# A gated linear attention with an FFN behind it: one table of calls in another order

## The chip, the cores and the metric

The kernel runs on one core of one Trainium2 chip. The metric is the device time of the whole program in microseconds, with smaller times better; it is compared by the median of several runs. Engines are named as in the profile: PE is TensorE, DVE is VectorE, ACT is ScalarE, POOL is GpSimd, and SP is SyncE, which does nothing here but start DMAs.

## The reference

The first half is a recurrence over 768 positions in each of 4 batches and 8 heads, with 48 complex gates per head. The second half is a plain FFN on its output.

```python
mag = np.sqrt(a_re * a_re + a_im * a_im)
scale = np.minimum(mag, 0.999) / (mag + 1e-06)
a_re_n, a_im_n = (a_re * scale, a_im * scale)
for t in range(S):
    S_re = ar * S_re - ai * S_im + kv      # kv = outer(k_t, v_t)
    S_im = ar * S_im + ai * S_re           # with the S_re of step t-1
    y[:, :, t] = einsum('bhd,bhde->bhe', q[:, :, t], S_re)
x = y.transpose(0, 2, 1, 3).reshape(B * S, H * D)     # 3072 x 384
h = x @ w_in                                          # 384 -> 2048
out = (h * (1.0 / (1.0 + np.exp(-h)))) @ w_out        # 2048 -> 384
```

## The kernel before

**Tiling.** The positions are cut into 24 chunks of 128, numbered n, in such an order that chunks n and n + 4 follow each other in the same batch. Two chunks make a pair p of 256 tokens, the unit of the FFN; there are 12 pairs. The FFN's 2048 columns are cut into 8 blocks jp.

**One chunk of attention.** The gates of a pair (logarithm of the magnitude, angle) come out of eleven steps G0 to Ga on ACT and DVE. The last of them, `gates_angle`, writes the tile th on the DVE (lines 431 and 433). For a chunk that has one before it in its batch, `carried` (line 441) adds the last row of the chunk before to th by an accumulating DMA on POOL's queue, th<-last. PE then forms running sums of both, ACT and DVE make sines, cosines and decays of them, and q and k are rotated and scaled on the DVE (line 551). `squared` (line 587) transposes the result in blocks of 32 into the tile sq, and `homed` (line 593) brings these blocks to their places in the tile T by twelve DMAs, T<-sq: six issued by SP and six by POOL. `weights` (line 606) multiplies a<-T on PE, `masked` (line 614) applies the causal mask on the DVE, and `output` (lines 633 and 636) gives y. `state` (lines 693 and 704) forms the chunk's contribution to the recurrent state, and `state_homed` (line 722) brings it into place by twelve more DMAs, S<-ssq, in the same way on both queues. `ends_of` stores a chunk's last decays by SP (line 522, ends<-eq) and loads them in another layout by two DMAs on POOL (line 525, dec<-ends), which wait for that store.

```python
def homed(n):
    to = home(n).rearrange("d w h a x -> d (w h) a x")
    for b in range(NB):
        for a in range(NA):
            (nc.gpsimd if a % 2 else nc.sync).dma_start(
                out=to[ts(b, Q), :, a],
                in_=X[n]["sq"][ts(a, Q), b].rearrange("p w h x -> p (w h) x"))
```

**One pair of the FFN.** `put` and `third_of` (lines 677, 681 and 645) bring y to the transposed input xT. From pair 3 on each product is split into three of lower precision: ACT makes the rounded copy xH of xT (`x_head`, line 772), the DVE the remainders xL and xD (lines 834 and 838), and `hidden` (line 762) multiplies xH by coarse, xL by fine and xD by mixed. For most blocks fine is loaded again by SP (`v_loaded`, line 817, fine<-w_firsts), and the DVE makes mixed of it and coarse (line 834). `silu` (line 312) gives g. ACT and DVE split g into head, tail and gd (lines 896, 834 and 838), and `result` (line 935; line 917 for the first pairs) multiplies them by three forms of w_out, one of which is loaded by SP (`w_loaded`, line 875, diff<-w_diffs). Loaded fine and diff tiles share a ring of three buffers; mixed has one.

**What sets the order.** The program is built by a table of calls, a string from line 1058 to 1204, in which each word is a call and its arguments: `td:18` is `homed(18)`, `xh:3` is `x_head(3)`, `h:6.1` is `hidden(6, 1)`. It runs under a manual schedule, so each engine and each queue executes its instructions exactly in the order in which the table issues them, and an instruction that waits holds back all those behind it on its engine or queue. Idle multiplications (`warm`) are calls of the table too; their results are not used. One thing depends on the order besides: ACT holds one set of function tables at a time. `special` (line 309) emits an ACT_TABLE_LOAD (line 306) when the set in place has not got the function that comes next.

Of the kernel before, what the change touches and what calls it, by code (L numbers as in the profile page):

```python
# [70 lines left out]
def kernel(  # L71
# [985 lines left out]
    with tc.manual_schedule():  # L1057
        for x in """
                warm:30 re:0 e0:0 im:0 e1:0 e2:0 re:1g im:1 e4:0 e0:1 im:2g e1:1 e3:0 im:3g e2:1
                e4:1 e6:0 e5:0 q:0g e6:1 e7:0 e7:1 e8:0 e8:1 L:0 re:2g e3:1 re:3g warm:20 exp:0  # L1060
                at:0.0 e5:1 F: L:1 an:0.0 at:0.1 v:0g phase:0 k:0g an:0.1 G0:1 phase:1 k:1g F: rd:0
                G5:1 R: v:2g turn:0 rd:1 trig:0 warm:34 turn:1 trig:1 dk:0 q:1g exp:1 G8:1 rk:0.0
                v:1g dq:0 rk:0.1 rq:0.0 H: G1:1 s:0 rq:0.1 dk:1 t:0.0 t:0.2 G7:1 ends:0 sm:1 J:
                T:0.0 T:0.2 last:0 t:0.1 dq:1 H: t:0.3 hold: rk:1.1 T:0.1 rq:1.1 G3:1 ends:1 q:2g
                rk:1.0 T:0.3 G6:1 w:0.1 t:1.1 m:0.1 G2:1 s:1 rq:1.0 G4:1 t:1.3 T:1.1 S:0 G9:1
                thirds:0 lk:1 w:0.0 L:3 exp:3 Ga:1 L:2 T:1.3 exp:2 t:1.2 phase:2 F: q:3g S:1 sm:0
                thirds:1 k:2g m:0.0 w:1.1 dq:2 rd:2 y:0 t:1.0 F: turn:2 trig:2 last:2 lk:0 H: im:4g
                dk:2 T:1.2 rq:2.0 rk:2.0 T:1.0 phase:3 rk:2.1 t:2.2 re:4g w:1.0 ends:2 F: R: x:0 R:
                rd:3 t:2.0 m:1.1 rq:2.1 T:2.0 turn:3 re:5g s:2 m:1.0 R: H: trig:3 y:1 k:3g F: T:2.2
                J: J: x:1 t:2.3 J: R: im:5g F: T:2.3 t:2.1 h:0.0 R: T:2.1 h:0.1 dq:3 S:2 rq:3.1  # L1070
                g:0.0 w:2.0 rq:3.0 dk:3 H: J: H: v:3g F: t:3.3 rk:3.1 t:3.2 rk:3.0 G0:2 w:2.1 G5:2
                G8:2 F: g:0.1 t:3.1 T:3.3 thirds:3 F: T:3.2 m:2.0 m:2.1 J: G1:2 H: thirds:2 t:3.0
                r:0.0 R: ends:3 J: T:3.0 R: y:2 H: T:3.1 H: last:1 x:2 G7:2 F: w:3.1 R: F: w:3.0
                G3:2 R: m:3.1 m:3.0 r:0.1 H: y:3 J: J: G2:2 J: x:3 R: F: v:4g G6:2 H: s:3 G4:2 F:
                G9:2 H: R: H: h:1.0 R: S:3 F: last:3 Ga:2 J: H: h:1.1 g:1.0 g:1.1 F: carried:4 J:
                R: L:4 R: r:1.0 F: J: r:1.1 h:1.2 h:0.2 phase:4 F: R: k:4g H: F: exp:4 J: H: J:
                g:1.2 R: R: sm:2 h:0.3 H: H: rd:4 F: carried:5 H: turn:4 J: g:0.2 F: R: F: q:4g J:
                h:1.3 trig:4 H: F: H: q:5g J: H: H: ends:4 R: F: J: J: dq:4 g:0.3 last:4 Q:4 lk:2
                R: dk:4 J: R: K:4 F: phase:5 r:1.2 H: L:5 R: rd:5 im:6g tk:4 g:1.3 R: r:0.2 turn:5
                F: h:1.4 J: H: exp:5 F: F: tq:4 k:5g H: J: R: g:1.4 h:0.4 R: J: J: J: H: g:0.4  # L1080
                r:0.3 h:1.5 R: R: h:0.5 ends:5 dq:5 H: J: J: wq:0 re:6g last:5 wq:1 wd:0 g:1.5
                r:1.3 g:0.5 im:7g ws:0 re:7g s:4 we:0 trig:5 wd:1 r:1.4 td:4 wq:2 dk:5 S:4 G0:3
                h:0.7 K:5 k:6g k:7g we:1 G5:3 Q:5 w:4.0 w:4.1 g:0.7 G1:3 h:0.6 tk:5 m:4.0 wk:0 tq:5
# [294 lines left out]
```

## Time and profile before

| | us |
|---|---|
| median of three runs (666.83 to 668.81) | 668.57 |
| the profiled execution, own time | 666.95 |
| its span | 665.2 |
| PE busy (92% of the span) | 613.8 |
| DVE busy (75%) | 495.6 |
| ACT busy (69%) | 458.0 |
| POOL busy (33%) | 222.4 |

The span is the time from the first to the last instruction in the profile; the execution's own time holds 1.75 us more around it. SP does nothing but start DMAs, which is not counted as busy. The granted clock of PE is given as a share of its full speed: 1.00 is 2.4 GHz and 0.50 is 1.2 GHz. In the lists of waits each line names the engine and line that waited, what released it, the us in total, the number of waits and the longest. In a timeline each line has its start in us from the span's start, the us it took, the engine, the line and the tiles (out<-in), with the idle time before it in brackets.

### The profile page before, as it was taken

What the parts mean: (1) busy time and instruction counts of PE and PEld (TensorE: products, weight loads), DVE (VectorE), ACT (ScalarE), POOL (GpSimd) and SP (SyncE); (2) the same over time, 40 slices, a digit from 0 to 9 for tenths busy, and PEclk for the clock granted to TensorE, in tenths of its full rate; (3) what the DMA queues carried; (4) which work ended last, traced back from release to release, by engine and by line L of the source; (5) the groups of instructions that cost most, each with busy time, mean ns of one, the idle gap of its engine ahead of it and who ended that gap; (6) DMA issues with size and microseconds to landing.
All of it is one profiled execution on the core that took longest, in us unless ns stands there. A gap on an engine that the chain in (4) does not pass through costs nothing.

```text
span 665.2 us, 12665 instructions
## 1 busy us (share of the span) xinstructions
PE 613.8 (92%) x4356; PEld 550.9 (83%) x4356; DVE 495.6 (75%) x763; ACT 458.0 (69%) x718; POOL 222.4 (33%) x389
## 2 busy tenths in 40 slices
PE   6799999999998797879899997999799999999995
PEld 4588777776887687869898997999799999999995
DVE  4879969885697898568799897688597887665353
ACT  7988856996999987537789677578568653343221
POOL 7242314462135422712442653225533033200000
PEclk8979999999999798989999998999799999999999
...
GB/s 177 178 85 204 188 257 169 139 174 213 170 194 225 177 178 143 189 180 157 177 180 151 181 122 223 115 191 158 128 114 220 199 187 160 157 231 156 184 147 95
DMA packets 168452, 114.27 MB, mean 172 GB/s; under 512 B 137804, under 2 KB 143504, under 8 KB 168384
## 3 DMA queue, kind: packets, MB, share of 16 engines
...
HBM read 83.50 MB, written 11.08 MB: 142 GB/s over the span
## 4 chain that ended last, share of the span: by engine, by line
PE 56%; ACT 19%; DMA 9%; DVE 6%; issue 6%; SPq 2%; POOL 1%; ACTq 0%; DVEq 0%; POOLq 0%
PE h L762 16%; PE o L935 16%; PE a L606 5%; PE h L755 4%; ACT L306 4%; ACT s L312 4%; PE o L917 4%; ACT mag L312 2%; PE y L633 2%; DMA T<-sq 2%; PE y L636 2%; DMA fine<-w_firsts 1%; ACT head L896 1%; PE s L693 1%; ACT g L312 1%
## 5 line engine op out<-in xcount | busy, mean ns | idle before, releaser
L593 POOL DMA_DIRECT2D T<-sq x120 | 70.8, 628 | 59.6 <-PE o L935 16.9
L306 ACT ACT_TABLE_LOAD x69 | 88.5, 1283 | 2.7 <-ACT ot L948 1.2
L312 ACT ACTIVATE g<-h 128x512 f32<-128x512 f32 x96 | 56.5, 594 | 45.2 <-PE h L762 34.5
L896 ACT ACTIVATE head<-g 128x512 fp32r<-128x512 f32 x75 | 47.2, 629 | 54.3 <-PE o L935 37.7
L525 POOL DMA_DIRECT2D dec<-ends x48 | 32.0, 694 | 156.0 <-DMA ends<-eq 149.8
L834 DVE SCALAR_TENSOR_TENSOR tail<-head,g 128x512 fp32r<-128x512 f32 x75 | 51.3, 684 | 42.5 <-ACT head L896 27.2
L762 PE MATMUL h<-xD,mixed 128*128 128x256 f32 x432 | 76.9, 287 | 5.0 <-DVE mixed L834 3.8
L762 PE MATMUL h<-xH,coarse 128*128 128x256 f32 x432 | 77.8, 289 | 2.0 <-ACT xH L772 1.4
L762 PE MATMUL h<-xL,fine 128*128 128x256 f32 x432 | 76.9, 287 | 1.4 <-DVE xL L834 1.4
L935 PE MATMUL o<-diff,gd 128*128 128x384 f32 x300 | 67.3, 346 | 5.1 <-DMA diff<-w_diffs 4.1
L606 PE MATMUL a<-T 96*128 96x128 f32 x384 | 56.5, 297 | 16.6 <-DMA xT<-y 4.2
L606 PEld LDWEIGHTS a<-T 96*128 96x128 f32 x384 | 52.7, 208 | 20.4 <-issue 8.5
L935 PE MATMUL o<-coarse,head 128*128 128x384 f32 x300 | 68.8, 351 | 0.4 <-ACT ot L948 0.4
L762 PEld LDWEIGHTS h<-xD,mixed 128*128 128x128 f32 x432 | 63.3, 194 | 6.1 <-DVE mixed L834 4.6
L762 PEld LDWEIGHTS h<-xH,coarse 128*128 128x128 f32 x432 | 64.2, 193 | 4.9 <-ACT g L312 2.0
L935 PE MATMUL o<-fine,tail 128*128 128x384 f32 x300 | 65.3, 340 | 0.3 <-DVE tail L834 0.3
L755 PE MATMUL h<-xT,w 128*128 128x256 f32 x288 | 65.3, 381 | 0.3 <-ACT g L312 0.2
L762 PEld LDWEIGHTS h<-xL,fine 128*128 128x128 f32 x432 | 63.2, 193 | 1.6 <-DVE xL L834 1.6
L755 PEld LDWEIGHTS h<-xT,w 128*128 128x128 f32 x288 | 54.0, 190 | 9.9 <-ACT g L312 1.8
L935 PEld LDWEIGHTS o<-diff,gd 128*128 128x128 f32 x300 | 53.3, 190 | 8.6 <-issue 4.5
L838 DVE SCALAR_TENSOR_TENSOR gd<-tail,g 128x512 fp32r<-128x512 f32 x75 | 51.5, 687 | 6.7 <-PE o L935 3.0
L722 POOL DMA_DIRECT2D S<-ssq x84 | 46.4, 614 | 27.4 <-DVE ssq L711 21.0
...
## 6 DMA issues: line engine op xcount, KB each, us to landing
...
```

The source lines that it names most:

```text
L306: nc.scalar.preload_act_table_set(SETS[of][0])
L312: nc.scalar.activation(out=out, in_=in_, func=func, **kw)
L525: nc.gpsimd.dma_start(out=x["dec"][a * D:(a + 1) * D], in_=ends[n].rearrange("(h d) -> d h", d=D))
L593: (nc.gpsimd if a % 2 else nc.sync).dma_start(out=to[ts(b, Q), :, a], in_=X[n]["sq"][ts(a, Q), b].rearrange("p w h x -> p (w h) x"))
L606: nc.tensor.matmul(ps[:, h], lhsT=x["kT"][hh * HH + h], rhs=x["qT"][hh * HH + h], start=True, stop=True)
L722: (nc.gpsimd if g % 2 else nc.sync).dma_start(out=to[ts(b, Q), r, :, e], in_=sq[ts(g, Q), :, b, 0:e.stop - e.start])
L755: nc.tensor.matmul(ps[:, ji], lhsT=of_first(w1, dc, jp * 2 + ji), rhs=A[p]["xT"][:, dc], start=(dc == 0), stop=(dc == ND - 1))
L762: nc.tensor.matmul(ps[:, ji], lhsT=w(dc, ji), rhs=x[:, dc], start=(f == 0 and dc == 0), stop=(f == len(forms) - 1 and dc == ND - 1))
L834: nc.vector.scalar_tensor_tensor(out=dst, in0=head.bitcast(F32), scalar=-FINER / MORE, in1=whole, op0=ALU.mult, op1=ALU.add)
L838: nc.vector.scalar_tensor_tensor(out=dst, in0=tail.bitcast(F32), scalar=MORE / FINER, in1=whole, op0=ALU.mult, op1=ALU.subtract)
L896: nc.scalar.mul(g_form(p, jp, "head"), A[p]["g", jp], MORE * SPLIT / FINER)
L935: nc.tensor.matmul(to, lhsT=left[:, ji, ts(m, C)], rhs=right(ji), start=(first_ and ji == 0 and n == 0), stop=(last_ and ji == 1 and n == 2))
```

## The change

The table's words are put in another order, from its first line to its last. No call is added, taken out or given another argument, and no buffer is changed. One line of it and one of the new order, the two in which `td:18` stands, show how they read:

```diff
@@ -1056,149 +1056,148 @@
-                carried:21 vx:6.6 gb:7.4 gc:7.4 g:6.5 x:17 ht:20 K:19 ut:20 r:7.4 td:18 dq:19 Q:19
...
+                exp:19 q:19 G1:10 g:6.4 h:7.4 k:19 lw:6.4 ends:19 td:18 G7:10 gr:7.3 w:17.1 vx:6.5
...
```

All engines get the same instructions but for the table loads of line 306, which follow from the order of ACT's functions: there were 69, and there are 73. Three places show how the rows moved. After a tile's name stands its number, and then its size; x6 is six DMAs in a row.

**POOL's queue, where chunk 18's tile T is filled.** T18<-sq18 are POOL's six of its twelve transfers, dec19 the loads of chunk 19's decays, th10 the angles of pair 10, and S20 and S21 states. Before:

```order
L722 DMA S21_5004<-ssq17_4946 32x4x16 x6
L441 DMA th10_4821<-last 1x16x24
L525 DMA dec19_5080<-ends 48x8x1 x2
L441 DMA th10_4821<-last 1x16x24
L593 DMA T18_5145<-sq18_5039 32x8x64 x6
L177 MEMSET v19_5220 128x16
```

And in the new order:

```order
L722 DMA S20_4855<-ssq16_4558 32x4x16 x6
L525 DMA dec19_4957<-ends 48x8x1 x2
L593 DMA T18_4960<-sq18_4878 32x8x64 x6
L441 DMA th10_4810<-last 1x16x24
L722 DMA S21_5156<-ssq17_4674 32x4x16 x6
L441 DMA th10_4810<-last 1x16x24
```

T18 went ahead of both accumulations into th10, and stands right behind the loads of dec19.

**SP's queue, where chunk 16's tile T is filled.** T16<-sq16 are SP's six transfers, S19<-ssq15 six of a state, fine6_1 a weight for block 1 of pair 6, and xT7 an FFN input. Before:

```order
L645 DMA xT7_4090<-y3_7_4092 16x256 x3
L875 DMA diff4_7_4291<-w_diffs 128x768
L497 DMA last<-turn17_4133 1x384
L722 DMA S19_4303<-ssq15_4125 32x4x32 x6
L522 DMA ends<-eq17_4296 1x384
L817 DMA fine6_1_4388<-w_firsts 128x768
L593 DMA T16_4396<-sq16_4153 32x8x64 x6
L817 DMA fine6_2_4415<-w_firsts 128x768
```

And in the new order:

```order
L645 DMA xT7_4124<-y3_7_4126 16x256 x3
L875 DMA diff4_7_4292<-w_diffs 128x768
L593 DMA T16_4303<-sq16_4178 32x8x64 x6
L497 DMA last<-turn17_4171 1x384
L722 DMA S19_4364<-ssq15_4061 32x4x32 x6
L817 DMA fine6_1_4399<-w_firsts 128x768
L181 DMA q17_4458<-in_q_dram 128x8x48
L875 DMA diff6_0_4491<-w_diffs 128x768
L522 DMA ends<-eq17_4359 1x384
L817 DMA fine6_2_4512<-w_firsts 128x768
```

T16 went ahead of S19, of the store ends<-eq17 and of fine6_1. On POOL, too, T16 went ahead of S19 and of dec17.

**ACT, from the copy of the FFN input xT3 to the rounded copy xH3.** s1_5, mag5 and th5 belong to the gates of pair 5, turn9 and cs9 to chunk 9, g2 and head2 to the FFN of pair 2. Before:

```order
L677 COPY xT3_1899<-y7_2024 128x3x128
L681 COPY y3_3_1901<-y7_2024 112x128
L896 ACTIVATE head2_6_2082<-g2_6_2015 128x512
L810 ACTIVATE coarse1_3_2047<-v_head7_1908 128x3x256
L312 ACTIVATE s1_5_2089<-re5_1838 128x768
L312 ACTIVATE s25_2090<-im5_1834 128x768
L312 ACTIVATE th5_2091<-re5_1838 128x768
L312 ACTIVATE g2_7_2100<-h2_7_1991 128x512
L306 ACT_TABLE_LOAD
L312 ACTIVATE s1_5_2089<-s1_5_2089 128x768
L312 ACTIVATE mag5_2102<-s1_5_2089 128x768
L772 ACTIVATE xH3_2125<-xT3_1899 128x768
```

And in the new order, from the row behind the copy xT3 on:

```order
L681 COPY y3_3_1770<-y7_2052 112x128
L312 ACTIVATE s1_5_2046<-s1_5_2046 128x768
L312 ACTIVATE mag5_2095<-s1_5_2046 128x768
L896 ACTIVATE head2_6_2102<-g2_6_1934 128x512
L312 ACTIVATE turn9_2113<-phase9_2080,round_b_110 128x384
L312 ACTIVATE mag5_2095<-mag5_2095 128x768 x2
L306 ACT_TABLE_LOAD
L312 ACTIVATE mag5_2095<-mag5_2095 128x768
L312 ACTIVATE cs9_2155<-turn9_2113 128x8x48 x2
L312 ACTIVATE cs9_2155<-cs9_2155,half_pi_b_108 128x8x48
L896 ACTIVATE head2_7_2159<-g2_7_2012 128x512
L772 ACTIVATE xH3_2164<-xT3_1768 128x768
```

Between xT3 and xH3 stand a turn, a second head and three more operations on mag5 and cs9 instead of a coarse, three of s and th, and a g.

On SP's queue a fourth place is touched, at the states S13 and S14. There diff3_6 and diff3_7 stood together behind both states; now diff3_6 stands ahead of S14, and diff3_7 behind S14, two loads of im7 and xT5. On POOL, S13 stands ahead of T11 now. At the start of the program the 34 idle multiplications `warm:34`, which stood behind `trig:0`, come ahead of the first running sum `L:0`, and `warm:20` behind `phase:1`.

## Rows read from the trace of the kernel before

**Rows 1.** The page: span, busy time (x instructions), granted PE clock in 40 slices

```profile
span 665.2 us, 12665 instructions
...
PE 613.8 (92%) x4356; PEld 550.9 (83%) x4356; DVE 495.6 (75%) x763; ACT 458.0 (69%) x718; POOL 222.4 (33%) x389
...
PEclk8979999999999798989999998999799999999999
```

**Rows 2.** PE's waits over the whole span: line, releaser, us in total, times, longest

```profile
PE a L606 <- DMA xT<-y: 4.2, 1, 4.2
PE o L935 <- DMA diff<-w_diffs: 4.1, 2, 3.9
...
PE L L460 <- DVE s L392: 3.4, 1, 3.4
PE a L606 <- issue: 3.3, 1, 3.3
```

**Rows 3.** The windows view by stretch: busy us (x instructions), granted clock, DMA share, GB/s

```profile
80.00:120.00 40.00, 39.82 (x167) 29.80 (x167) 32.36 (x60) 24.70 (x41) 14.47 (x20) 1.00 0.87 211
120.00:160.00 40.00, 39.61 (x220) 28.76 (x219) 31.07 (x39) 33.67 (x48) 18.22 (x28) 1.00 0.62 160
160.00:216.70 56.70, 52.04 (x326) 44.04 (x324) 39.63 (x57) 55.13 (x84) 21.46 (x39) 1.00 0.75 202
216.70:225.50 8.80, 5.35 (x30) 4.63 (x32) 7.67 (x9) 8.70 (x14) 2.11 (x5) 0.61 0.60 142
410.20:416.60 6.40, 6.38 (x24) 6.40 (x25) 4.23 (x7) 2.76 (x6) 0.53 (x2) 0.50 0.73 184
473.10:478.10 5.00, 5.00 (x23) 5.00 (x24) 4.18 (x6) 1.78 (x4) 3.17 (x6) 0.50 0.23 29
478.10:600.00 121.90, 121.12 (x966) 116.77 (x965) 90.44 (x133) 66.68 (x112) 32.40 (x60) 1.00 0.70 181
```

**Rows 4.** The timeline of POOL, 446 to 468 us: start, us, instruction, idle before

```profile
448.96 3.27 POOL L722 DMA_DIRECT2D S<-ssq  x6 [10.18 <-DVE ssq L711]
459.93 0.84 POOL L441 DMA_DIRECT2D th<-last  x1 [7.70 <-ACT head L896]
460.47 1.61 POOL L525 DMA_DIRECT2D dec<-ends  x2
461.75 1.19 POOL L441 DMA_DIRECT2D th<-last  x1
462.29 4.15 POOL L593 DMA_DIRECT2D T<-sq  x6
```

**Rows 5.** The timeline of DVE around 454 and 458 us

```profile
453.41 0.93 DVE L587 STREAM_TRANSPOSE sq<-qr 128x768 f32<-128x768 f32 x1
...
458.42 0.96 DVE L433 SCALAR_TENSOR_TENSOR th<-mag,re 128x768 f32<-128x768 f32 x1
```

**Rows 6.** The timeline of SP's queue, 390 to 404 us

```profile
392.68 4.56 SPq L722 DMA_DIRECT2D S<-ssq  x6
...
397.82 0.35 SPq L817 DMA_DIRECT2D fine<-w_firsts  x1
398.47 3.88 SPq L593 DMA_DIRECT2D T<-sq  x6
```

**Rows 7.** The timeline of SP's queue, 276 to 292 us

```profile
281.50 7.68 SPq L722 DMA_DIRECT2D S<-ssq  x12
289.27 1.01 SPq L875 DMA_DIRECT2D diff<-w_diffs  x2
```

**Rows 8.** The page's costliest groups: ACT's table loads (busy us, mean ns, idle before)

```profile
L306 ACT ACT_TABLE_LOAD x69 | 88.5, 1283 | 2.7 <-ACT ot L948 1.2
```

**Rows 9.** The timeline of ACT, 207 to 219 us

```profile
213.75 1.28 ACT L306 ACT_TABLE_LOAD   x1
215.04 0.85 ACT L312 ACTIVATE s<-s 128x768 f32<-128x768 f32 x1
...
216.67 0.83 ACT L772 ACTIVATE xH<-xT 128x768 fp32r<-128x768 f32 x1
```

More of the change, by code (lines that the diff above doesn't have):

```diff
@@ L1058 @@
         for x in """
[L1059 to L1081, printed above, removed]
@@ L1196 @@
[L1196 to L1201 removed]
+                re:0 im:0 e0:0 e1:0 warm:30 e2:0 im:1 e4:0 re:1g e0:1 e6:0 e7:0 e1:1 e2:1 warm:34
@@ new lines @@
+                e3:0 e5:0 re:2g e8:0 e4:1 e6:1 im:2g L:0 e3:1 exp:0 im:3g q:0g e5:1 e7:1 at:0.0
+                re:3g e8:1 an:0.0 at:0.1 k:0g L:1 dk:0 an:0.1 phase:0 G0:1 phase:1 k:1g rd:0 dq:0
+                v:0g rd:1 turn:0 q:1g trig:0 turn:1 trig:1 F: G5:1 warm:20 F: rq:0.0 exp:1 rk:0.0
+                hold: last:0 G8:1 rq:0.1 rk:0.1 t:0.2 H: v:1g G1:1 k:2g t:0.3 sm:0 G7:1 q:2g T:0.3
+                dq:1 dk:1 t:0.0 T:0.2 s:0 rq:1.1 G2:1 t:0.1 rk:1.1 ends:0 T:0.0 t:1.3 w:0.0 F:
+                rq:1.0 G3:1 T:1.3 H: G4:1 T:0.1 G6:1 G9:1 lk:0 L:2 t:1.1 exp:2 rk:1.0 w:0.1 m:0.0
@@ new lines @@
+                last:12 xt:4 gc:3.6 oc:2.1 vx:4.0 xd:5 im:15 ut:13 trig:12 r:3.6 xg:4 lw:3.7
+                phase:13 hl:13 gr:3.7 xh:5 gb:3.7 h:4.0 gc:3.7 dk:12 ul:13 xt:5 s:11 ends:12 re:15
+                xg:5 K:12 r:3.7 rd:13 h:5.0 lv:4.1 turn:13 L:13 q:12 vx:4.1 g:4.0 oc:2.0 G0:7 g:5.0
+                gr:4.0 h:4.1 dq:12 lw:4.0 tk:12 gb:4.0 oc:3.1 G8:7 h:5.1 gc:4.0 Q:12 lv:4.2 tq:12
+                g:4.1 r:4.0 g:5.1 gr:5.0 k:13 gb:5.0 gc:5.0 q:13 v:12 oc:3.0 lw:4.1 G5:7 exp:13
+                vx:4.2 r:5.0 gr:4.1 gb:4.1 h:5.2 G1:7 G7:7 gc:4.1 G2:7 td:12 r:4.1 k:14 gr:5.1
@@ new lines @@
+                h:5.6 tk:15 w:14.1 gb:4.5 exp:16 last:15 carried:17 lw:4.5 gc:4.5 carried:16 tq:15
+                sm:6 sd:13 w:14.0 ht:16 m:14.1 ut:16 lv:4.7 r:4.5 m:14.0 gr:5.5 xd:6 gb:5.5
+                phase:16 gc:5.5 vx:4.7 td:15 lk:6 r:5.5 gr:4.6 lk:7 s:15 rd:16 turn:16 S:13 ss:15
+                gb:4.6 ht:17 ends:16 g:5.6 S:12 h:4.7 xh:6 g:4.7 trig:16 xt:6 y:14 re:18 x:14
+                w:15.0 w:15.1 dk:16 lw:4.6 last:16 im:18 im:19 gc:4.6 ut:17 K:16 m:15.0 r:4.6
+                phase:17 hl:17 m:15.1 rd:17 dq:16 gr:5.6 lv:6.0 tk:16 y:15 ul:17 k:17 Q:16 x:15
@@ new lines @@
+                tq:16 re:19 h:5.7 turn:17 gb:5.6 gc:5.6 sd:14 r:5.6 xg:6 G0:9 g:5.7 L:17 v:16
+                gr:4.7 xd:7 G5:9 G1:9 xh:7 gb:4.7 vx:6.0 gc:4.7 lw:4.7 s:16 td:16 G7:9 r:4.7 gr:5.7
+                G2:9 h:6.0 xt:7 last:17 gb:5.7 exp:17 xg:7 sd:15 h:7.0 G8:9 gc:5.7 lv:6.1 G3:9
+                r:5.7 g:6.0 w:16.0 vx:6.1 trig:17 G6:9 m:16.0 G4:9 h:6.1 gr:6.0 gb:6.0 g:7.0 q:17
+                oc:4.1 g:6.1 oc:4.0 h:7.1 G9:9 gc:6.0 lw:6.0 r:6.0 ends:17 dk:17 lv:6.2 oc:5.1
+                vx:6.2 Ga:9 gr:6.1 k:18 oc:5.0 gb:6.1 h:6.2 lw:6.1 K:17 carried:18 gc:6.1 hl:18
```

235 lines of the change are left out of this document (116 added, 119 removed).

## The prediction

> **What bounds the kernel now.** I read the busy shares first, then what TensorE (PE) waited for, then the stretches around its longest waits, and last the queues and engines that released them. The page shows PE busy 613.8 of 665.2 us, with ScalarE (ACT) at 69% and VectorE (DVE) at 75% [rows 1]. An average of 92% says that only PE's idle time and its slow-clock time can be saved, because the change takes no multiplication away. Seven of the 40 slices have a granted clock under 9 tenths (the 1st, 3rd, 14th, 16th, 18th, 25th and 29th) [rows 1]. The list of PE's waits then gives four single waits of over 3 us: 4.2 before an attention product a<-T, 3.9 before a second FFN product that needs diff<-w_diffs, 3.4 at the start (L<-s), and 3.3 before another a<-T [rows 2]. Each is one place in the order.
>
> The stretches show what such a wait costs besides itself. After the wait that ends at 410.2, PE worked 6.40 us at a granted clock of 0.50, that is at 1.2 instead of 2.4 GHz; after the one that ends at 473.1, 5.00 us at 0.50 [rows 3]. Work at half the clock takes twice its time, so these two waits cost another 3.2 and 2.5 us. From 478.1 to 600 PE is busy 121.12 of 121.90 us at clock 1.00 [rows 3]: there is nothing to gain late in the program.
>
> One stretch has another limit. From 160 to 216.7 us ACT is busy 55.13 of 56.70 us, while PE has 52.04; in the next 8.8 us PE is busy only 5.35, with ACT at 8.70 [rows 3]. There the order of ACT's own work decides.
>
> **The change, part by part.** All calls are kept; their order differs on each engine and queue. So there are no removed or added operations to price, with one exception (below), and I price the places at which PE waits.
>
> *The transfers T18 (second a<-T wait).* Tile T18 is filled from sq18 by twelve DMAs, six issued by SP and six by POOL. The DVE wrote sq18 by 453.41 + 0.93 = 454.34 [rows 5]. POOL had been idle for 7.70 us when it went on at 459.93, with the accumulation th10<-last, which waits for the DVE's th of 458.42 to 459.38 [rows 4, 5]. After it came two loads of dec19, a second accumulation, and only then, at 462.29, T18's six issues of 4.15 us [rows 4]. PE's wait of 4.2 us follows [rows 2]. (The row names xT<-y; that transfer is issued behind T18 on this queue, and these multiplications read only T18.) In the new order T18 stands before both accumulations, so POOL need not wait for th. It still waits for dec19, which needs a small store on SP first. The 7.70 us of idle time may shrink by anything from nothing to all; I take 3 us, since the store follows on DVE's work of just before 454. With that, and as the two accumulations (0.84 and 1.19 us) lie behind T18 now, it is issued about 5 us sooner. That alone is more than 4.2. Besides, PE's calls between the transposition of sq18 and the product that needs T18 grow from 14.6 us to about 26 us, by the durations of the same calls now. I take the whole wait and its slow clock: -4.2 - 2.5 = **-6.7**. The ends are 0 (something else on that queue is late) and -6.7. What is late next is th10, the angle for pair 5, which is put back by T18's 4.15 us; the first user is ACT, before two later chunks, and POOL is idle afterwards, so I cost it at nothing, and at 4 us if ACT has no work before it.
>
> *The transfers T16 (the wait of 3.3).* On SP these six issues (3.88 us from 398.47) stood behind S19's six (4.56 us from 392.68) and behind fine6_1 at 397.82 [rows 6]. In the new order they come before S19. That saves 4.56 us and more on SP, and on POOL the wait for dec17. The whole of it would be -3.3 - 3.2 = -6.5. But fine6_1, which the hidden products of pair 6 need, is now behind T16 and S19: 3.88 + 4.56 = 8.4 us of issues from about 393.5 put it at some 402, 4.2 us later than 397.82, and the hidden product h:6.1 needs one more DVE operation on it. PE comes there at about the same point of its work. Between no new wait and one of 4.2 us I take the upper part, 4.0, for this product: -6.5 + 4.0 = **-2.5**, with ends 0 and -6.5.
>
> *The transfers diff3_6 and diff3_7 (the wait of 3.9).* Before, SP issued S13 and S14, twelve DMAs in 7.68 us from 281.50, and then both diffs at 289.27 [rows 7]. Now S13 is earlier, and diff3_6 comes before S14; but diff3_7 comes behind S14, behind two loads and behind xT5, which waits for an attention output. So one wait goes (-3.9) and half of it is likely to come back at diff3_7 (+0.9 to +3). On POOL, T11 now stands behind S13, and the margin that its product had is about the length of six such issues (3.27 us) [rows 4]: +1.5, half of it. The small loads of the next pair are later too: +1. Net **-0.5**, with ends -3.9 and +3.
>
> *The rounded copy xH3 on ACT.* xH3 starts pair 3's hidden products, and is copied at 216.67 [rows 9]. In the new order more of ACT's work stands between the first silu of pair 2 and xH3: one table load (1.28 us), eight operations of 128x768 at 0.85 us [rows 9], and eleven of about half that width, which I put at 0.5 us: 1.28 + 6.8 + 5.5 = 13.6 us. PE's work ahead of pair 3's first product grows too, by 5.2 us (from 48.8 to 54). At worst PE waits 13.6 - 5.2 = 8.4 us more there. But ACT has that work behind it afterwards, and has less up to xH4; so most of it only changes places. The nearest piece, from the copy xT3 to xH3, is 1.5 us longer on ACT, and PE has 2.6 us more to do meanwhile, a gain of 1.1 if nothing else is late. I take **+1.5**, with ends -1.1 and +8.4.
>
> *Four more table loads.* Whether ACT must load a function table depends on the order of its functions: the order has 73 loads in place of 69. The page has 1283 ns for each [rows 8], so 4 x 1.28 = 5.1 us of ACT. They fall mostly between 80 and 160 us, where ACT is busy 24.70 and 33.67 of 40 us [rows 3] and PE 39.82 and 39.61, so PE's own work covers them unless the loads stand before something that PE awaits. I take **+1**, ends 0 and +5.1. A load starts at 213.75, takes 1.28 us, and the next operation starts at 215.04, 0.01 us behind its end [rows 9]. The Trainium skill (page "ScalarE: Activation LUTs", section "What ACT_TABLE_LOAD costs") has some 1380 ns of DRAIN on top of each load, 2.66 us in all. By it the four loads would be 10.6 us in place of 5.1; the trace does not show that gap.
>
> *The start.* A group of idle multiplications, which keep PE's clock up, moves ahead of the first running sum, where PE waited 3.4 us [rows 2]. That fills the wait, but ACT and DVE set the pace there. **0**, ends -3.4 and, by one chunk's transfers coming late, +5.
>
> **The sum.** -6.7 - 2.5 - 0.5 + 1.5 + 1 + 0 = -7.2 us. The profiled execution took 666.95 us (span 665.2 and 1.75 around it), which is 1.62 below the median of 668.57. So 666.95 - 7.2 = 659.75, and on the scale of the median about 661.4; I say **661.5**. A change of 0.3%, 2.0 us, is about what a measurement of this kernel can tell from none.
>
> **The rivals.** First, all three places could come out whole: -6.7 - 6.5 - 3.9 = -17.1, or 651.5 us on the median's scale. For it speaks that each wait is one late transfer; against it, that fine6_1 and diff3_7 are put behind the very transfers that were late.
>
> Second, the gains could be eaten before they are made. The T18 and T16 waits lie after 400 us, and PE reaches them later if the stretch up to 220 us gets longer: xH3 with +6.3, three quarters of its end, in place of +1.5, and the loads with +3 in place of +1, give -7.2 + 4.8 + 2 = -0.4, or 668.2 us, no change that can be told.
>
> Third, and slower than before: ACT becomes the bound up to xH3. The mechanism is the backlog of 13.6 us of ACT work before xH3, less the 5.2 us of PE's, with the four loads (5.1 us) in the same engine's way: 8.4 + 5.1 = 13.5 us lost. It decides from the point where this loss is above what the three places give, 6.7 + 2.5 + 0.5 = 9.7 us. Then the sum is +3.8 us, or 672.4 us. For it speaks that ACT has no idle time at all to speak of from 160 to 216.7 us [rows 3]; against it, that ACT's work is the same in sum except for the loads, and that 80 to 160 us have room for some of it.
>
> That the change does not do what it says is a small case: the calls are the same, but not the instructions, by the four loads; they are in the sum.
>
> **How the numbers follow.** The forecast has a chance of 0.42. The first rival (651.5) has 0.18, the second (no change) 0.16, the third (672.4) 0.24. Faster by over 0.3% is the forecast and the first rival: 0.60. Within 0.3% is 0.16, slower 0.24. The range goes from 649, which takes in the first rival and a small gain at the start, to 674, which takes in the third with a little beyond it. Alone, the forecast's own cases go from 656 to 665.
>
> **What would show it.** Right: PE's waits of 4.2 and 3.3 us before a<-T are gone, with no stretch at clock 0.50 after them; POOL issues T18 right after dec19; a new wait of 1 to 4 us stands at a hidden product near 400 us; ACT has 73 loads from line 306. Wrong for T18 if POOL sits idle before dec19 until about 460. For rival three, PE's first product of pair 3 is over 8 us later than 217 with PE idle ahead of it. The forecast falls if the span less PE's busy time, 665.2 - 613.8 = 51.4 us now, comes out no smaller.

## The result and the profile after

| | before | new order |
|---|---|---|
| median, us | 668.51 | 648.33 |
| runs, us | 666.83 to 668.81 | 647.99 to 652.64 |
| profiled execution, own time, us | 666.95 | 648.07 |
| its span, us | 665.2 | 646.3 |

The ratio is 0.9718, with a 95% interval of 0.9674 to 0.9762: the new order is faster by 20 us, where 7 were forecast, and 0.7 us faster than the range allowed. In the profiled executions the difference is 18.9 us. Runs that lie more than 1.5% above the fastest of their kernel are left out of medians and ratios, here and in the experiments.

The page of the new order, in the parts of [rows 1] and [rows 8]:

```profile
PE 604.0 (93%) x4356; PEld 543.4 (84%) x4356; DVE 493.9 (76%) x763; ACT 461.7 (71%) x722; POOL 223.6 (35%) x389
...
PEclk9789999999999899979999999999999999999999
...
L306 ACT ACT_TABLE_LOAD x73 | 93.7, 1283 | 2.8 <-ACT ot L948 1.2
```

PE is busy 9.8 us less than before with the same multiplications. Nothing was taken out: busy time multiplied by the granted clock of the whole execution is 613.8 x 0.965 = 592.3 us before and 604.0 x 0.980 = 591.9 now. So the 9.8 us are work that runs at the full clock now. The span less PE's busy time went from 51.4 to 42.3 us, 9.1 less. The gain is thus about half waiting and half slow clock, and the forecast had priced slow clock at two places only. There are 73 table loads, as counted.

PE's waits in the new order (line, releaser, us in total, times, longest), for [rows 2]:

```profile
PE phase L460 <- DVE th L433: 3.6, 2, 2.5
PE o L935 <- DVE gd L838: 3.1, 5, 1.0
...
PE a L606 <- DMA fine<-w_firsts: 2.7, 1, 2.7
```

The waits of 4.2 (a<-xT), 3.9 (o<-diff) and 3.3 us (a<-issue) are gone. The longest behind the first 50 us is a new one of 2.7 us, before w:11.0. (Its row names fine<-w_firsts, but these multiplications read only the tile T11.)

To see where the time went I take PE's lost time in a stretch: its length less PE's busy time multiplied by the granted clock. Idle time and slow clock are both in it. Each figure comes from one execution, and as the clock has two digits here, it is good to about 0.3 us in most stretches. The columns of the windows view are those of [rows 3]. Before:

```profile
160.00:234.00 74.00, 64.60 (x403) 55.03 (x402) 54.58 (x78) 71.40 (x107) 28.58 (x51) 0.95 0.76 198
234.00:300.00 66.00, 55.51 (x456) 50.81 (x455) 50.26 (x74) 42.21 (x68) 24.46 (x44) 0.95 0.73 171
400.00:450.00 50.00, 46.13 (x334) 43.73 (x333) 36.36 (x55) 34.27 (x55) 14.84 (x27) 0.93 0.72 173
450.00:500.00 50.00, 45.52 (x371) 43.40 (x370) 38.68 (x57) 34.56 (x54) 23.61 (x43) 0.93 0.61 132
```

The new order, in the same stretches:

```profile
160.00:234.00 74.00, 63.32 (x389) 53.66 (x388) 55.08 (x78) 69.64 (x105) 22.58 (x39) 0.95 0.71 194
234.00:300.00 66.00, 62.08 (x514) 57.65 (x513) 55.31 (x83) 47.15 (x78) 29.43 (x52) 0.95 0.77 189
400.00:450.00 50.00, 48.15 (x392) 46.08 (x390) 41.67 (x63) 42.39 (x63) 18.85 (x35) 1.00 0.75 176
450.00:500.00 50.00, 48.40 (x383) 46.11 (x384) 41.85 (x62) 37.18 (x59) 21.88 (x40) 1.00 0.69 173
```

The first row before gives 74 - 64.60 x 0.95 = 12.6 us lost, and in the new order 74 - 63.32 x 0.95 = 13.8. All stretches, with the differences beside what the forecast had for them:

| us from the start | before | new order | difference | forecast |
|---|---|---|---|---|
| 0 to 52 | 16.9 | 16.9 | 0.0 | 0 |
| 52 to 160 | 0.6 | 1.0 | +0.4 | +1 (loads) |
| 160 to 234 | 12.6 | 13.8 | +1.2 | +1.5 (xH3) |
| 234 to 300 | 13.3 | 7.0 | -6.3 | -0.5 (diffs, T11) |
| 300 to 400 | 4.3 | 3.8 | -0.5 | |
| 400 to 450 | 7.1 | 1.9 | -5.2 | -2.5 (T16) |
| 450 to 500 | 7.7 | 1.6 | -6.1 | -6.7 (T18) |
| 500 to 550 | 0.8 | 0.0 | -0.8 | |

That sums to -17.3 of 18.9 us. The stretches are cut by time, so the new order is a little further along in the later ones; after 500 us there is nothing left to lose in either, and this cannot change the sum much. The forecast was near at the start, the loads, xH3 and T18's stretch. It missed the stretch from 234 to 300 us by 5.8 us, and T16's by 2.7.

Four places in the new order's timelines. POOL's queue around T18, for [rows 4]:

```profile
437.50 1.27 POOL L525 DMA_DIRECT2D dec<-ends  x2 [8.77 <-DMA ends<-eq]
438.76 3.46 POOL L593 DMA_DIRECT2D T<-sq  x6
445.89 0.83 POOL L441 DMA_DIRECT2D th<-last  x1 [3.67 <-ACT s L312]
```

T18 is issued at 438.76, right behind dec19, and th10<-last stands after it, so its wait of 3.67 us no longer holds T18 up.

SP's queue around T16, for [rows 6], and then PE at the hidden product h:6.1:

```profile
382.91 3.94 SPq L593 DMA_DIRECT2D T<-sq  x6
...
387.40 4.94 SPq L722 DMA_DIRECT2D S<-ssq  x6
392.44 0.53 SPq L817 DMA_DIRECT2D fine<-w_firsts  x1
```

```profile
395.77 0.62 PE L762 MATMUL h<-xL,fine 128*128 128x256 f32 x3 [1.39 <-DMA fine<-w_firsts]
396.84 0.62 PE L762 MATMUL h<-xD,mixed 128*128 128x256 f32 x3 [0.44 <-DVE mixed L834]
```

T16 stands ahead of S19 now, and fine6_1 goes out at 392.44, behind both. PE waits 1.39 us for it and 0.44 us for the mixed made from it, where the forecast had 4.0, and its clock stays at 1.00 from 394.4 to 406 us.

SP's queue around diff3_6 and diff3_7, for [rows 7]:

```profile
273.50 0.56 SPq L875 DMA_DIRECT2D diff<-w_diffs  x1
...
276.26 4.26 SPq L722 DMA_DIRECT2D S<-ssq  x6
...
289.68 0.52 SPq L875 DMA_DIRECT2D diff<-w_diffs  x1
```

diff3_6 is issued at 273.50 in place of 289.27, and diff3_7 at 289.68, hardly earlier than before; and yet no product waits for it in this execution.

ACT up to xH3, for [rows 9], and PE at the product that the head before it feeds:

```profile
220.10 1.28 ACT L306 ACT_TABLE_LOAD   x1
221.39 0.84 ACT L312 ACTIVATE mag<-mag 128x768 f32<-128x768 f32 x1
...
223.62 0.61 ACT L896 ACTIVATE head<-g 128x512 fp32r<-128x512 f32 x1
224.14 0.83 ACT L772 ACTIVATE xH<-xT 128x768 fp32r<-128x768 f32 x1
```

```profile
224.28 1.65 PE L935 MATMUL o<-coarse,head 128*128 128x384 f32 x4 [1.34 <-ACT head L896]
...
228.01 0.51 PE L762 MATMUL h<-xH,coarse 128*128 128x256 f32 x3
```

xH3 is copied at 224.14, 7.5 us later than before. PE does not wait for it: in the new order r:2.7 stands ahead of the first product of pair 3, and its wait of 1.34 us is for a head. The first product of pair 3 starts at 228.01, 10.5 us later than before (217.55), behind PE waits of 1.17, 0.97 and 1.34 us: that is the sign that the prediction put down for its third rival. But the loss up to 234 us is only 1.2 us larger, because in the kernel before PE waits at this product and right behind it (1.43, 1.38 and 1.22 us, for xH, xL and xD), with slow clock after that. The table load of 1.28 us at 220.10 is again followed by the next operation 0.01 us behind it.

### The profile page after: what moved, and what is told of

It is laid out like the page before. It is cut to its first block, busy times and chain, and to the rows that moved or that the text cites. A ratio compares the mean times of both kernels' runs of the same rounds, so it can differ in the third digit from the quotient of the medians.

```text
span 646.3 us, 12653 instructions
## 1 busy us (share of the span) xinstructions
PE 604.0 (93%) x4356; PEld 543.4 (84%) x4356; DVE 493.9 (76%) x763; ACT 461.7 (71%) x722; POOL 223.6 (35%) x389
## 3 DMA queue, kind: packets, MB, share of 16 engines
q0 software_dynamic: 12288, 17.23, 13.5%
## 5 line engine op out<-in xcount | busy, mean ns | idle before, releaser
L762 PE MATMUL h<-xH,coarse 128*128 128x256 f32 x432 | 76.4, 285 | 1.3 <-ACT g L312 1.2
L762 PE MATMUL h<-xL,fine 128*128 128x256 f32 x432 | 75.3, 282 | 1.4 <-DMA fine<-w_firsts 1.4
L762 PEld LDWEIGHTS h<-xH,coarse 128*128 128x128 f32 x432 | 62.9, 188 | 3.7 <-ACT g L312 2.0
L762 PEld LDWEIGHTS h<-xD,mixed 128*128 128x128 f32 x432 | 61.6, 189 | 4.1 <-DVE mixed L834 3.2
L755 PEld LDWEIGHTS h<-xT,w 128*128 128x128 f32 x288 | 54.1, 190 | 12.4 <-ACT g L312 2.6
L762 PEld LDWEIGHTS h<-xL,fine 128*128 128x128 f32 x432 | 61.5, 188 | 1.6 <-DMA fine<-w_firsts 1.6
L606 PE MATMUL a<-T 96*128 96x128 f32 x384 | 53.8, 289 | 4.2 <-DMA fine<-w_firsts 2.7
L935 PEld LDWEIGHTS o<-fine,tail 128*128 128x128 f32 x300 | 53.3, 190 | 4.9 <-DVE tail L834 4.6
L606 PEld LDWEIGHTS a<-T 96*128 96x128 f32 x384 | 51.0, 203 | 7.3 <-issue 3.0
L834 DVE SCALAR_TENSOR_TENSOR mixed<-fine,coarse 128x768 fp32r<-128x768 f32 x40 | 38.1, 952 | 24.9 <-PE h L762 13.5
```

The lines of the kernel that those rows point to most:

```text
L606: nc.tensor.matmul(ps[:, h], lhsT=x["kT"][hh * HH + h], rhs=x["qT"][hh * HH + h], start=True, stop=True)
L755: nc.tensor.matmul(ps[:, ji], lhsT=of_first(w1, dc, jp * 2 + ji), rhs=A[p]["xT"][:, dc], start=(dc == 0), stop=(dc == ND - 1))
L762: nc.tensor.matmul(ps[:, ji], lhsT=w(dc, ji), rhs=x[:, dc], start=(f == 0 and dc == 0), stop=(f == len(forms) - 1 and dc == ND - 1))
L834: nc.vector.scalar_tensor_tensor(out=dst, in0=head.bitcast(F32), scalar=-FINER / MORE, in1=whole, op0=ALU.mult, op1=ALU.add)
L935: nc.tensor.matmul(to, lhsT=left[:, ji, ts(m, C)], rhs=right(ji), start=(first_ and ji == 0 and n == 0), stop=(last_ and ji == 1 and n == 2))
```

## The experiments

The diffs show the lines of the table, wrapped as before; where two orders are joined, the table stands as a list of words, for short. All medians are of at least four runs, and each kernel was measured beside runs of before, whose medians were 668 to 670 us. The ratio is not the quotient of the two medians given with it, from which it differs by up to 0.3%. Single executions spread more there than in the first measurement: 31 runs of before went from 665.45 to 673.12 us. For the small effects I therefore read the lost time of the stretch as well as the total. (The expectations took the lost time from the single records, which gives 13.9 us where the windows view gives 13.3.)

### One place at a time

The three places of the forecast, each made alone in the table of before. T18:

```diff
-                gc:6.4 Ga:10 h:7.5 carried:20 w:17.1 dk:19 ends:19 r:6.4 m:17.1 y:17 gr:7.4
-                carried:21 vx:6.6 gb:7.4 gc:7.4 g:6.5 x:17 ht:20 K:19 ut:20 r:7.4 td:18 dq:19 Q:19
+                gc:6.4 Ga:10 h:7.5 td:18 carried:20 w:17.1 dk:19 ends:19 r:6.4 m:17.1 y:17 gr:7.4
+                carried:21 vx:6.6 gb:7.4 gc:7.4 g:6.5 x:17 ht:20 K:19 ut:20 r:7.4 dq:19 Q:19
```

> The table of before with one word moved: td:18 from behind r:7.4 to ahead of carried:20. Theory A (each late transfer is a loss of its own): the wait of 4.17 us before w:18.1 and the 2.5 us of slow clock behind it go, 6.7 us, about 662 us beside a before of 668.5. Rival E (what is saved there is waited for at the next late thing, so that only the whole new order keeps it): less than 3 us, and another wait of over 2 us within 30 us behind it.

Measured: 667.26 us beside 669.64, ratio 0.9966 (0.9930 to 1.0001). That is 2.4 us, not 6.7, and the interval reaches from 4.7 us less to none. PE's waits of over 1 us behind 470 us, from its timeline:

```profile
476.00 0.88 PE L704 MATMUL s<-kr,v 128*64 128x96 f32 x16 [1.17 <-ACT L L312]
...
488.51 2.12 PE L606 MATMUL a<-T 96*128 96x128 f32 x16 [1.78 <-DMA im<-in_a_im_dram]
```

The wait before w:18.1 is gone. But now w:19.1 waits 1.78 us for the next tile, T19, and a state product waits 1.17 us for ACT. The stretch from 450 to 500 us loses 3.3 us in place of 7.7:

```profile
450.00:500.00 50.00, 46.74 (x400) 44.44 (x398) 40.48 (x60) 36.52 (x56) 25.43 (x46) 1.00 0.67 142
```

So rival E has a part, though the next wait is 1.78 us and not the 2 that it asked for: about 4.4 us of 6.7 stay in this stretch, and the next late transfer takes most of the rest. POOL shows why T19 is late. Its six issues stand behind two loads of the next decays, which wait for a store that SP issues only at 475.59:

```profile
478.23 1.41 POOL L525 DMA_DIRECT2D dec<-ends  x2 [7.80 <-issue]
479.76 3.45 POOL L593 DMA_DIRECT2D T<-sq  x6
```

T16:

```diff
-                exp:17 tq:16 last:17 gc:4.7 sd:15 G7:9 xh:7 ends:17 h:6.0 r:4.7 G2:9 xt:7 xg:7
+                exp:17 tq:16 last:17 gc:4.7 td:16 sd:15 G7:9 xh:7 ends:17 h:6.0 r:4.7 G2:9 xt:7 xg:7
...
-                gr:5.7 G4:9 G3:9 gb:5.7 h:7.0 dk:17 lv:6.1 gc:5.7 g:6.0 G6:9 td:16 vx:6.1 trig:17
+                gr:5.7 G4:9 G3:9 gb:5.7 h:7.0 dk:17 lv:6.1 gc:5.7 g:6.0 G6:9 vx:6.1 trig:17
```

> The table of before with one word moved: td:16 to ahead of sd:15. Theory A: the wait of 3.29 us and the 3.2 us of slow clock go, and a hidden product of pair 6 waits about 1.4 us for fine6_1, as in the trace of the new order: -5 us, about 663.5 us. The forecast had -2.5 (a new wait of 4 us). Rival E: less than 2 us.

Measured: 670.34 us beside 669.64, ratio 1.0038 (1.0008 to 1.0068). Nothing is gained, as rival E had it; if anything the kernel is slower. The wait for T16 has become one for fine6_1 at the hidden product:

```profile
410.39 1.01 PE L762 MATMUL h<-xL,fine 128*128 128x256 f32 x3 [2.87 <-DMA fine<-w_firsts]
```

This is the new wait that the forecast named, 2.87 us, and it takes nearly all of the 3.29. From 400 to 450 us the loss is 50 - 46.55 x 0.93 = 6.7 us in place of 7.1, about the same:

```profile
400.00:450.00 50.00, 46.55 (x335) 44.35 (x334) 37.28 (x56) 35.46 (x56) 16.73 (x31) 0.93 0.69 172
```

The two loads diff3_6 and diff3_7:

```diff
-                lw:3.5 g:3.7 ht:13 w:11.0 gb:3.5 w:11.1 sd:9 gc:3.5 sd:10 m:11.1 lk:5 lw:3.6 m:11.0
+                lw:3.5 g:3.7 ht:13 w:11.0 gb:3.5 w:11.1 lw:3.6 sd:9 gc:3.5 lw:3.7 sd:10 m:11.1 lk:5 m:11.0
```

(lw:3.7 is taken out of its old place in the next line.)

> The table of before with lw:3.6 moved ahead of sd:9 and lw:3.7 ahead of sd:10, so that each load stands ahead of one of the two states on SP. The forecast had -0.5 for this place as the new order has it. Theory A: the wait of 3.93 us and 1.7 us of slow clock go, 5.6 us, about 663 us. Rival F (the states S13 and S14, put back by it, or T11 become late, or the ring of three buffers holds the loads): less than 2 us.

Measured: 664.26 us beside 669.64, ratio 0.9936 (0.9899 to 0.9973): 4.3 us less by the ratio, 5.4 by the medians. The stretch from 234 to 300 us loses 66 - 59.20 x 0.97 = 8.6 us in place of 13.3:

```profile
234.00:300.00 66.00, 59.20 (x490) 53.90 (x490) 53.60 (x79) 44.19 (x71) 25.68 (x46) 0.97 0.73 177
```

SP's queue in this kernel:

```profile
281.10 0.81 SPq L875 DMA_DIRECT2D diff<-w_diffs  x2
...
285.88 0.54 SPq L875 DMA_DIRECT2D diff<-w_diffs  x1
286.46 3.83 SPq L722 DMA_DIRECT2D S<-ssq  x6
```

diff3_6 goes out in the row at 281.10, with the load ahead of it, and diff3_7 at 285.88 between the two states. No wait of 1 us or more is left at either, nor at T11. Theory A holds here, and the forecast's -0.5 does not.

One thing more stands in this execution. The order around T16 is that of before, and yet PE waits only 1.71 us for T16 in place of 3.29, and the stretch from 400 to 450 us loses 3.2 us in place of 7.1. What a late transfer costs thus depends on more than the order next to it, and a difference of 4 us in that stretch, between single executions, does not by itself show what a moved word did.

### The places together, and two words more

The three edits in one table:

> The table of before with the three edits of the single experiments together: td:18, td:16, and lw:3.6 with lw:3.7. Theory A2 (these places are worth together about what their own stretches showed: 5.4 us from 234 to 300, 1.1 around 410 and 3.6 around 480): -10 us, about 659 us beside a before of 669; the other half of the new order's 20 us is then elsewhere. Rival B3 (they were worth little one by one because each uncovered the next; together they give nearly all): 653 us or less.

Measured: 665.18 us beside 667.87, ratio 0.9940 (0.9896 to 0.9984): 2.7 us less by the medians, 4.0 by the ratio. Neither theory had so little. In the profiled execution, which was the fastest of its ten runs, the stretch from 234 to 300 us loses 8.6, as with the diffs alone. From 350 to 400, 400 to 450 and 450 to 500 us it is 4.3, 3.3 and 4.8, 12.4 together in place of 16.9; with the diffs alone they were 1.6, 3.2 and 7.9, 12.7 together. So these executions do not show that moving T16 and T18 gained anything on top of the diffs. The wait for fine6_1 stands there with 3.43 us, and that for T19 with 2.11:

```profile
PE h L762 <- DMA fine<-w_firsts: 3.4, 1, 3.4
...
PE a L606 <- DMA im<-in_a_im_dram: 2.1, 1, 2.1
```

(The second row names a load of im; the product is w:19.1, which reads only T19.) If the next late transfers are what the rest of the new order settles, two more words must bring what is missing there:

```diff
-                exp:17 tq:16 last:17 gc:4.7 td:16 sd:15 G7:9 xh:7 ends:17 h:6.0 r:4.7 G2:9 xt:7 xg:7
+                exp:17 tq:16 last:17 gc:4.7 td:16 lv:6.1 sd:15 G7:9 xh:7 ends:17 h:6.0 r:4.7 G2:9 xt:7 xg:7
...
-                gr:7.5 gb:7.5 gc:7.5 ends:20 rd:21 r:7.5 xt:8 g:7.6 hl:21 td:19 g:6.7 gr:6.6 m:18.0
+                gr:7.5 gb:7.5 gc:7.5 td:19 ends:20 rd:21 r:7.5 xt:8 g:7.6 hl:21 g:6.7 gr:6.6 m:18.0
```

(lv:6.1 is taken out of its old place as well.)

> The three places together, with two words more moved: lv:6.1 right behind td:16 (ahead of the state S19), and td:19 ahead of ends:20. Theory U (each of the moved transfers uncovered the next late one of its queue, and the whole new order is worth more because it moves these too): the wait of 3.43 us before the hidden product of pair 6 and that of 2.11 us before w:19.1 go, with 1.6 and 1.7 us of slow clock: about 8 us less than three_places between 395 and 490 us, 656 to 659 us. Rival V (other waits take their place, and the rest of the new order is needed for other reasons): less than 4 us of the 8, 662 us or more.

Measured: 660.28 us beside 668.93, ratio 0.9884 (0.9846 to 0.9923). The stretches from 350 us on:

```profile
350.00:400.00 50.00, 47.83 (x419) 45.81 (x418) 43.78 (x65) 39.20 (x63) 25.75 (x47) 0.97 0.71 156
400.00:450.00 50.00, 48.54 (x369) 45.42 (x369) 40.99 (x63) 39.12 (x60) 16.23 (x30) 1.00 0.70 174
450.00:500.00 50.00, 49.19 (x407) 46.45 (x406) 42.00 (x62) 38.87 (x63) 24.34 (x44) 1.00 0.79 171
```

They lose 3.6, 1.5 and 0.8 us: 5.9, which is what the new order loses there (2.4 + 1.9 + 1.6 = 5.9), and 6.5 less than with three places. Both waits are gone, and no wait of 0.5 us or more is left between 395 and 500 us. Theory U holds for this part of the program: the few words moved do there what the whole new order does. The total came out 1 to 4 us above its expectation, between the two theories; in this execution the stretches up to 350 us lost 2 us more than with three places, at the same order.

### Half of one order and half of the other

These kernels take the order of one table up to a call, and then all calls that are left in the order of the other:

```diff
-table = before
+table = before[:before.index(cut)] + [call for call in new if call is left]
```

The cut is at h:1.0:

> The table of before up to the call h:1.0 (about 73 us), then all other calls in the new order. Theory A (the gain is made place by place, in each stretch as the idle and slow-clock time of PE there differs between the two traces): this takes back 0.5 us of 20, so about 649 us. Rival B (the early part of the program, idle multiplications and clock included, sets up what comes later): it takes back several us, 652 or more.

At L:7:

> The order of before up to the call L:7 (about 151 us), then the new order. Theory A: about 649 us, since the two traces hardly differ up to there. Rival C (the forecast's: four table loads between 80 and 160 us cost something there): 648 or less, since the new order's loads of that stretch are gone.

At h:3.2:

> The order of before up to h:3.2 (about 234 us), then the new order. Theory A: the new order lost 3 us more of PE's time between 160 and 230 us (xH3 and the results of pair 2 wait for ACT), so this is faster than the new order by about 2.3 us: 646 us. Rival C (that loss is given back by less work on ACT right after): 648 to 649 us.

At h:4.0:

> The order of before up to h:4.0 (about 299 us), then the new order. Theory A: the stretch from 230 to 300 us was worth 7.8 us (waits of 2.75, 1.84, 1.07 and 3.93 us with their slow clock), so the time is about 654 us. Rival B2 (the two late tiles T16 and T18 are nearly the whole gain, as the forecast's second case had it, and the middle is worth the 0.5 us of the forecast): about 649 us.

And two the other way round, with the new order first, cut at h:3.2 and at h:4.0:

> The new order up to h:3.2 (about 237 us in its own trace), then the order of before. Theory P (the new order has ACT and DVE do work ahead of pair 3's first product, loses 3 us of PE there, and is repaid from 234 to 300 us): PE's idle and slow time from 234 to 300 us falls from 13.9 to 9 us or less although the order there is that of before, and the total is 665 to 668 us. Rival S (the gain from 234 to 300 comes from the order within that stretch): 13 us or more from 234 to 300, and a total of 669 to 672 us.

> The new order up to h:4.0 (about 289 us in its own trace), then the order of before. Theory A2: the early and middle part bring their 6 to 9 us, and the losses of before around 410 and 480 us come back with its order (over 10 us of idle and slow time from 400 to 500): 660 to 663 us. Rival T (T16 and T18 are late because of what lies before 300 us): 655 us or less, with under 6 us of idle and slow time from 400 to 500.

Measured, beside a before of 670.41 (first four) and 667.87 us (the other two), with the lost time in the stretches; the last row is the first measurement's:

| kernel | us | ratio (interval) | 160 to 234 | 234 to 300 | 400 to 500 |
|---|---|---|---|---|---|
| before | | | 12.6 | 13.3 | 14.8 |
| before up to h:1.0, then new | 644.13 | 0.962 (0.955 to 0.969) | 12.8 | 1.8 | 4.4 |
| before up to L:7 | 652.26 | 0.974 (0.968 to 0.981) | 18.2 | 3.4 | 7.4 |
| before up to h:3.2 | 653.85 | 0.978 (0.970 to 0.986) | 12.2 | 12.8 | 6.5 |
| before up to h:4.0 | 661.79 | 0.988 (0.981 to 0.995) | 13.3 | 16.0 | 7.4 |
| new up to h:3.2, then before | 662.43 | 0.991 (0.987 to 0.996) | 13.5 | 12.2 | 11.5 |
| new up to h:4.0, then before | 661.18 | 0.990 (0.986 to 0.993) | 17.3 | 9.0 | 11.0 |
| new order | 648.33 | 0.972 (0.967 to 0.976) | 13.8 | 7.0 | 3.5 |

- The gain lies on both sides of 300 us: by the medians the new order behind h:4.0 alone brings 8.6 us, and ahead of it alone 6.7. Rival B2, that T16 and T18 are nearly all, falls. So does rival T, since the losses from 400 to 500 us come back with before's order (11.0). But theory A, which adds up place by place, had 654 us for the cut at h:4.0 and misses by 8: there the stretch from 234 to 300 us lost 16.0 us with before's order in it, and that from 400 to 500 us 7.4, more than the new order's 3.5.
- The stretch from 234 to 300 us is better only where the order inside it is new (1.8, 3.4, 7.0, and 9.0 with the new order up to 290; with the cut at h:3.2 it is new too, but loses 12.8 by a wait of 5.65 us for a diff, close behind the seam); it stays at 12.2 with the new order only ahead of it. So theory P falls, that ACT's work moved ahead of xH3 is repaid there. The total of that kernel was lower than either theory had it.
- The seams cost something of their own. With the cut at L:7 the stretch from 160 to 234 us loses 18.2, more than either order, and with the cut at h:3.2 there is the wait of 5.65 us. These kernels show where the gain lies, not its exact size. The cuts at L:7 and h:3.2 were expected at 646 to 649 us and came out at 652 and 654; these two losses are a part of that.
- The first is faster than the new order itself, which neither theory had. Its start loses no less (17.4 us up to 52 us, against 16.9); it lacks the wait before w:11.0, and its stretch from 234 to 300 us is the best of all:

```profile
234.00:300.00 66.00, 64.20 (x551) 60.36 (x550) 60.19 (x90) 50.69 (x83) 31.67 (x57) 1.00 0.85 207
```

The new order again, beside the same runs of before as the kernel with six words moved:

> The new order itself, unchanged, beside the same runs of before as five_places. If the wait of 2.7 us before w:11.0 with its slow clock belongs to the order it is there again and the time is about 648 us (as measured before); if it is a coincidence of transfers it is under 1 us, and the time is about 644 us, as with the old start.

Measured: 648.69 us, ratio 0.9722 (0.9660 to 0.9785), as before. The wait is there again, in PE's timeline, now with 3.46 us:

```profile
280.55 2.42 PE L606 MATMUL a<-T 96*128 96x128 f32 x16 [3.46 <-issue]
```

So it belongs to the order, together with its own start: it stands in all three executions whose table is new from the beginning up to here (2.68, 3.46, and 2.84 us with the new order up to h:4.0), and with the old start up to h:1.0 or L:7 at most 0.35 us of it, though the queues have the same order there. In the first two POOL issues one of T11's transfers (270.29 and 270.52), stops for 0.77 us, and has issued the last at 274.57 and 274.79; with the old start up to h:1.0 it issues six in a row from 269.12 to 272.62. What holds them has not been found.

### Filling a wait

In `weights`, multiplications whose result the real ones overwrite:

```diff
+        any_ = upto_r.bitcast(mybir.dt.bfloat16)
+        for _ in range({(16, 1): 52, (18, 1): 66}.get((n, hh), 0)):
+            nc.tensor.matmul(ps[:, 0], lhsT=any_[:, 0:C], rhs=any_[:, 0:C], start=True, stop=True)
         for h in range(HH):
```

> The order of before, with 52 idle multiplications of 128 columns ahead of w:16.1's own and 66 ahead of w:18.1's, into the tile that these overwrite, so that PE works during most of its two waits for T16 and T18. The waits themselves stay. Theory G (PE's slow clock behind a wait comes from the wait): the 3.2 and 2.5 us at a granted clock of 0.50 behind them go, 5.7 us, about 663 us. Rival H (the slow clock comes of something else there, as the transfers): no change, 668.5 us.

Measured: 666.56 us beside 669.64, ratio 0.9953 (0.9921 to 0.9985), 3.1 us less. The two places before:

```profile
406.00:420.00 14.00, 10.71 (x60) 10.53 (x60) 8.38 (x13) 5.73 (x10) 4.99 (x8) 0.76 0.72 193
468.00:485.00 17.00, 12.83 (x84) 12.29 (x84) 10.21 (x17) 9.46 (x15) 9.87 (x18) 0.80 0.68 135
```

And with the waits filled:

```profile
406.00:420.00 14.00, 13.32 (x127) 12.22 (x126) 10.09 (x15) 12.63 (x19) 6.36 (x10) 1.00 0.82 209
468.00:485.00 17.00, 17.00 (x174) 16.58 (x174) 11.81 (x19) 10.88 (x19) 10.27 (x19) 1.00 0.81 174
```

PE is at clock 1.00 through both, in place of 0.76 and 0.80. The waits themselves are filled, not shorter: idle multiplications count as busy here. Theory G holds at the place. The total shows 3.1 of 5.7 us, with an interval of 1.0 to 5.3; the profiled execution, the slowest of its ten runs, had 3.3 us more lost between 234 and 300 us, and 5.7 more from 300 to 400, where its order is that of before.

The same at the start, in the table that is old up to h:1.0 (48 idle multiplications ahead of w:0.1's own):

```diff
+        for _ in range(48 if (n, hh) == (0, 1) else 0):
```

> The order of before up to h:1.0 and then the new order, as in the first experiment, with 48 idle multiplications of 128 columns ahead of w:0.1's own, so that PE works through its wait of 3.1 us at 28 us. Theory G: the stretch at a granted clock of 0.50 from 31 to 41 us, which costs 5 us, gets shorter by half or goes: 639 to 642 us, beside 644 without it. Rival H (that stretch comes of something else, as the work's kind): 644 us and the same stretch.

Measured: 640.17 us (637.58 to 640.63), ratio 0.9575 to the before of 667.87 beside it (0.9518 to 0.9632), where without the filling it was 644.13 and 0.962 (0.955 to 0.969), beside 670.41. From 26 to 42 us, first without it and then with it:

```profile
26.00:42.00 16.00, 12.88 (x69) 11.21 (x68) 12.78 (x22) 13.12 (x20) 6.07 (x10) 0.68 0.48 132
```

```profile
26.00:42.00 16.00, 14.25 (x145) 11.81 (x143) 14.96 (x26) 15.79 (x25) 7.08 (x12) 1.00 0.51 136
```

The clock goes from 0.68 to 1.00. On 12.88 us of busy time that is 12.88 x 0.32 = 4.1 us; the medians differ by 4.0 us. Against its own before each, it is 3 us by the ratios, whose intervals overlap, and 1.4 us by the medians: the clock of the stretch shows the effect, and the total does not settle its size. This is the fastest version here, 28 us below the before beside it and 8 below the new order.

## Why the prediction was wrong

**The sum was 7 where 20 were measured.** The sign and the kind of places were right. The first rival (all three places whole, 651.5 us) was near in size, but not in its reason: the three places moved by themselves gave 3 to 4 us of its 17. Two steps failed above all, both between 234 and 300 us: the diffs were priced at -0.5, and the smaller waits there were put at nothing. By its steps:

- **T18, -6.7.** 6.1 us were saved in that stretch. But the reason given was incomplete, so that the size is partly luck. T18 alone brings 2.4 us in the total and 4.4 in its stretch, because T19 comes late next. The step "what is late next is th10" named the wrong transfer: the new order also puts td:19 ahead of ends:20, and the forecast had not looked at it.
- **T16, -2.5.** 5.2 us. But the stretch lost 3.9 and 3.6 us less also where the order around T16 is that of before (with the diffs alone, and with the new order only up to h:3.2), so how much of the 5.2 is T16's own move is open. The feared wait for fine6_1 is real: moved alone, T16 gains nothing, for fine6_1 takes 2.87 us. In the new order it is 1.39 and 0.44 us, without slow clock behind it. The term of 4.0 us was too large by 2.2 us. It put T16's issues at about 393.5 and fine6_1 at 402, and assumed that PE comes there at the same point of its work. But T16 is issued from 382.91 in the new order, 15.6 us earlier than before, and fine6_1 at 392.44, while h:6.1 starts only 10.7 us earlier (393.77 against 404.51).
- **The diffs, -0.5: the first step that failed.** The wait at diff3_6 was worth 4.7 us with its slow clock in its own stretch, and 4.3 in the total, when moved alone. The term left out the slow clock behind this wait (clock 0.57 over 3.76 us, 1.6 us). What came back at diff3_7 was taken at 0.9 us in the sum, though the text says half of 3.9. In the new order nothing came back: diff3_7 is issued at 289.68, and r:3.7, which starts at 291.94, multiplies by two other forms first. But PE comes late to r:3.7 there because of T11. In three executions with that order there and the old start up to h:1.0 or L:7, where T11's wait is missing or 0.35 us, the same product does wait for its diff, 0.24, 0.27 and 1.49 us, the last with the start filled. T11 did become late, and that cost more than the +1.5 put for it: 2.68 us and slow clock behind it (0.50 over 3.46 us), some 5 us by the stretch, 7.0 against 1.8.
- **Waits that were not in the sum at all: the second step that failed.** From 234 to 300 us before had four more waits (0.51, 2.75, 0.76 and 1.84 us), which the forecast put at nothing by leaving them as they are. The two long ones, and the one for diff3_6:

```profile
252.79 1.01 PE L762 MATMUL h<-xD,mixed 128*128 128x256 f32 x3 [2.75 <-DVE mixed L834]
...
270.38 1.21 PE L606 MATMUL a<-T 96*128 96x128 f32 x8 [1.84 <-ACT L L312]
...
293.24 1.18 PE L935 MATMUL o<-diff,gd 128*128 128x384 f32 x4 [3.93 <-DMA diff<-w_diffs]
```

  Behind the wait of 2.75 us the clock was 0.50 for 3.21 us; behind that of 1.84 it stayed at 1.00. In the new order no wait of this stretch but T11's is above 0.50 us; in the kernel without T11's wait the stretch loses only 1.8 us in all, 6.8 less than with the diffs alone. By these differences between single executions, -4.7 for the diffs, -6.8 for the rest of the stretch, these waits above all, and +5.2 for T11 make its -6.3, where -0.5 was forecast. Which moved words removed the four waits has not been tested.
- **xH3, +1.5.** +1.2, at 7.5 us later on ACT. Right in size, but partly by luck: PE waits for a tail, a gd and a head there (1.17, 0.97 and 1.34 us), and not for xH3. Rival three falls: its sign, a late first product of pair 3, came, but it cost no more than these 1.2 us, and ACT is busy 69.64 of the 74 us in place of 71.40.
- **Loads, +1, and start, 0.** +0.4 and 0.0.

The range ended at 649, because only the three priced places could come out better; small waits that nobody had priced had no room in it.
